# Attention steps of two batches placed in the middle of units and outputs, and their kv one unit later

## The chip, the cores and the metric

The kernel runs on one core of one Trainium2 chip. The metric is the device time in microseconds (us). A run also has a *span*, from the first to the last instruction of its trace; in most runs here the device time is 1.7 to 1.9 us above the span. "Fast" runs alone are compared. In the profile's lines PE is TensorE's products and PEld its weight loads, DVE is VectorE, ACT is ScalarE, POOL is GpSimd, and L158 is line 158 of that run's kernel.

## The reference, cut to what matters

```python
def _attn_ref(q, k, v, g_norm):            # q, k, v: 8 batches x 8 heads x 576 tokens x 64
    kv  = np.einsum('bhsd,bhse->bhde', k, v)
    out = np.einsum('bhsd,bhde->bhse', q, kv)
    rms = np.sqrt(np.mean(out * out, axis=-1, keepdims=True) + 1e-06)
    return out / rms * g_norm
# its result, as x of 4608 tokens x 512, goes through
def _moe_ref(x, w_a, w_b, w_out):          # d_ff = 1536
    return ((x @ w_a) * (x @ w_b)) @ w_out
```

Nearly all the arithmetic is in the three large products. The attention is small, but every token of x has to pass through it first.

## The kernel before

The 4608 tokens go through the large products in nine strips of 512 (`s` = 0 to 8). A strip has 12 *units* (`ffn_ab`: part a with 4 products and a ScalarE copy, part b with 4 products and a VectorE multiplication) and then 4 *outputs* (`ffn_o`: 12 products each). In strip `s`, the attention of batch `b = s + 1` is computed in *slots* between units and outputs, so that its x is ready when strip `s + 1` wants it. A batch has 4 pairs of heads, and a pair goes through these steps:

- `kv`: 40 narrow products for all four pairs at once, then `kv_out`, two ScalarE copies (their result is `kvb`);
- `x`: two 288-column products into banks 4 and 5 of PSUM, the memory that the products write to, then `psq`, the ScalarE square (its result is `sq`);
- `pss`: two 288-column products of the squares into banks 6 and 7, then ScalarE's reciprocal root (`rs`); and `pst`: two VectorE products that read banks 4 and 5 and write x.

All pairs (0 to 3) use the same banks 4 and 5, so x of one pair must wait for pst of the pair before it.

```python
    X, SS = (4, 0), 6
    # class Attn, cut
        def psq(self, p, i0):
            nc.scalar.activation(sq[p % 3], P[:, i0 : i0 + 2, 0:HF], AF.Square)
        def pss(self, p, i0, hs=(0, 1)):
            ...  # two products into banks i0, i0 + 1, then rs on ScalarE
        def pst(self, p, x0, hs=(0, 1)):
            for h in hs:
                ...
                nc.vector.scalar_tensor_tensor(out=xt[p][:, t0 : t0 + HF],
                    in0=P[:, x0 + h, 0:HF], scalar=g_col, in1=rs[p % 3][:, h, :], ...)
        def x(self, p, i0):
            for h in range(2):
                nc.tensor.matmul(P[:, i0 + h, 0:HF], lhsT=kvb[self.b % 2][:, p, :], ...)

    def slot(A, s, n):
        kb = P[:, 7, 0 : NP * D].rearrange("q (p e) -> q p e", e=D)
        k0, kn, xs = (5, 1, (7, 9, 11, 13)) if s < 3 else (2, 1, (4, 7, 10, 12))
        if k0 <= n < k0 + kn:
            for p in range((n - k0) * NP // kn, (n - k0 + 1) * NP // kn):
                A.kv(p, kb[:, p, :])
            if n == k0 + kn - 1:
                A.kv_out(slice(0, NP), kb)
        for p in range(NP):
            if n == xs[p]:
                A.x(p, X[0])
                A.psq(p, X[0])
            if n == xs[p] + 1:
                A.pss(p, SS)
                A.pst(p, X[0])

    for s in range(1, N_STRIP - 1):
        b = s + 1
        A = Attn(b) if b < B else None
        for n in range(FC + 4):
            if n >= FC:
                i = O if n % 2 == 0 else n_ab[0] % 3
                n_ab[0] += n % 2
                ffn_o(s, n - FC, i)
            elif s > 1 or n > 1:
                ffn_ab(s, n)
            if A:
                slot(A, s, n)
            ...  # loads of later batches
```

Of the kernel before, what the change touches and what calls it, by code (L numbers as in the profile page):

```python
# [15 lines left out]
def kernel(  # L16
# [18 lines left out]
    FC = d_ff // 128  # L35
    NP = H // 2
# [59 lines left out]
    O = 3  # L96
# [26 lines left out]
    def load_late(b):  # L123
        if b > EARLY:

            nc.gpsimd.tensor_copy(gate, qT[(b - 1) % 2][0:1, 0, 0:1])  # L126
        d = qs_d[b].rearrange("t (h d) -> t h d", h=H)
        for hs in (slice(0, NP), slice(NP, H)):
            nc.gpsimd.dma_start(out=d[:, hs, :], in_=q[b, hs].rearrange("h t d -> t h d"))  # L129
        n = 128 * LC  # L130
        for t, src in ((ktl[b % 2], k), (vtl[b % 2], v)):
            nc.gpsimd.dma_start(
                out=t[:, :, 0:LC, :],
                in_=src[b, :, 0:n].rearrange("h (t c) d -> t h c d", c=LC),
            )
            nc.gpsimd.dma_start(
                out=t[0 : S - n, :, LC, :], in_=src[b, :, n:].rearrange("h t d -> t h d")
            )

    def transpose_q(b):  # L140
        nc.sync.dma_start_transpose(qT[b % 2], qs_d[b])
# [102 lines left out]
    class Unit:  # L244
        n = 0
# [32 lines left out]

    n_ab = [0]

    def ffn_ab(s, fc):
        i = n_ab[0]
        n_ab[0] += 2
        Unit(s, fc, i % 3, (i + 1) % 3).rest()

    def store(t0, t, e0, e1, eng=nc.sync):
        i = 0
# [15 lines left out]
    def o_mm(s, g, i, fcs, e0=0, e1=d_model):  # L303
        for fc in fcs:
            nc.tensor.matmul(  # L305
                P[:, i, e0:e1],
                lhsT=abt[s % 2][fc][:, g * 128 : (g + 1) * 128],
                rhs=wo_t[:, fc, e0:e1],
                start=(fc == 0),
                stop=(fc == FC - 1),  # L310
            )

    def o_out(s, g, i):
        n = n_o[0]
        n_o[0] += 1
        t = o_sb[n % 4]
        if n % 2:
            nc.scalar.copy(t, P[:, i, :])  # L318
        else:
            nc.vector.tensor_copy(t, P[:, i, :])  # L320
        store(s * STRIP + g * 128, t, 0, d_model)

    def ffn_o(s, g, i=O):
        o_mm(s, g, i, range(FC))
        o_out(s, g, i)


# [41 lines left out]
    X, SS = (4, 0), 6  # L369


    A = Attn(0)
# [31 lines left out]
    for p in range(1, NP):  # L404
        i = X[p % 2]
# [38 lines left out]
    for fc in range(4, FC):  # L444
        ffn_ab(0, fc)


    A = Attn(1)
    h1, h2 = range(0, FC // 2), range(FC // 2, FC)

    nc.sync.dma_start(out=gate_d, in_=vt[1][0:1, H - 1, EC - 1, D - 1 : D])
    ffn_o(0, 0, X[0])
    pieces = [(1, h1), (1, h2), (2, h1), (2, h2), (3, h1), (3, h2)]
    for n, (g, fcs) in enumerate(pieces):
# [24 lines left out]
    def slot(A, s, n):  # L479

        kb = P[:, 7, 0 : NP * D].rearrange("q (p e) -> q p e", e=D)
        k0, kn, xs = (5, 1, (7, 9, 11, 13)) if s < 3 else (2, 1, (4, 7, 10, 12))
        if k0 <= n < k0 + kn:
            for p in range((n - k0) * NP // kn, (n - k0 + 1) * NP // kn):
                A.kv(p, kb[:, p, :])
            if n == k0 + kn - 1:
                A.kv_out(slice(0, NP), kb)
        for p in range(NP):
            if n == xs[p]:
                A.x(p, X[0])  # L490
                A.psq(p, X[0])
            if n == xs[p] + 1:
                A.pss(p, SS)
                A.pst(p, X[0])

    for s in range(1, N_STRIP - 1):
        b = s + 1
        A = Attn(b) if b < B else None
        for n in range(FC + 4):
            if n >= FC:  # L500
                i = O if n % 2 == 0 else n_ab[0] % 3
                n_ab[0] += n % 2
                ffn_o(s, n - FC, i)
            elif s > 1 or n > 1:
                ffn_ab(s, n)
            if A:
                slot(A, s, n)
            if n == 8 and b + 1 < B:
                if s > 1:
                    transpose_q(b + 1)  # L510
                    if b + 2 < B:
                        load_late(b + 2)
                else:
                    load_late(3)
        if s == 1:
            transpose_q(3)
            load_late(4)
    last = N_STRIP - 1
    for fc in range(FC):
        ffn_ab(last, fc)  # L520
    for g in range(3):
        ffn_o(last, g, (O, 4)[g % 2])
# [38 lines left out]
```

## Time and profile before

| | before |
|---|---|
| device time, median of 3 runs (range) | 322.15 us (321.6 to 322.46) |
| span of the profiled run | 320.7 us |
| PE busy, share of the span | 98% |
| VectorE, ScalarE busy | 39%, 39% |
| granted TensorE clock | 1.0 |

The head of the page of the kernel before: busy time with its share of the span and the number of instructions, and the granted clock in 40 slices (9 is 90% or more).

```profile
span 320.7 us, 4732 instructions
PE 315.0 (98%) x1883; PEld 150.6 (47%) x1883; DVE 124.9 (39%) x218; ACT 125.5 (39%) x217; POOL 70.0 (22%) x94
PEclk9999999999999999999999999999999999999999
```

PE busy at 98% does not yet say that PE is at its best. In this trace the records of products overlap: one 512-column product is recorded with 379 ns, but the next one starts 216 ns after it. The first line is that of one of the three large products in the kernel before (busy us, mean ns of one, idle us before), the other two are from its timeline (start us, duration us):

```profile
L255 PE MATMUL P<-xt,wa_t 128*128 128x512 bf16 x432 | 111.9, 379 | 0.0
64.17 1.03 PE L255 MATMUL P<-xt,wa_t 128*128 128x512 bf16 x4
65.03 1.03 PE L255 MATMUL P<-xt,wb_t 128*128 128x512 bf16 x4
```

Four products start in 65.03 - 64.17 = 0.86 us. So the question to put to each place is whether the *starts* follow each other at that rate. They do nearly everywhere. The exceptions can be found in two views. The first is PE's waits in the kernel before: who waited for whom, in total, how often, the longest.

```profile
PE P L330 <- DVE eps_t L345: 1.2, 1, 1.2
PE P L158 <- DMA vtl<-in_v_dram: 0.5, 1, 0.5
PE P L209 <- ACT sq L205: 0.4, 1, 0.4
```

The first and third are at the start, as is a fourth line of 0.2 us that is left out. The second is kv of batch 2, in strip 1, waiting for the tile `vtl` with v. The timeline of the kernel before shows it (start, duration, engine, line, what was done, how many; in brackets the idle time before it and who ended it):

```profile
60.07 1.03 PE L255 MATMUL P<-xt,wb_t 128*128 128x512 bf16 x4
61.03 0.32 PE L158 MATMUL P<-vtl,ktl 128*64 128x64 bf16 x8
61.80 0.69 PE L158 MATMUL P<-vtl,ktl 128*64 128x64 bf16 x32 [0.46 <-DMA vtl<-in_v_dram]
62.43 1.04 PE L255 MATMUL P<-xt,wa_t 128*128 128x512 bf16 x4
```

From the first kv product to the next unit's first product it takes 62.43 - 61.03 = 1.40 us. The same group in strip 2 takes 0.75 us, so 0.64 us is lost here (1.397 - 0.754 by the unrounded starts):

```profile
95.81 0.82 PE L158 MATMUL P<-vtl,ktl 128*64 128x64 bf16 x40
96.56 0.61 PE L255 MATMUL P<-xt,wa_t 128*128 128x512 bf16 x2
```

The second exception is too small for the view of waits. This is the timeline of the kernel before around x of pair 1 in strip 1:

```profile
67.86 0.41 PE L209 MATMUL P<-sq,ones 128*128 128x288 bf16 x2
68.31 0.74 ACT L213 ACTIVATE rs<-P,eps_t 128x576 f32<-128x576 f32 x1 [0.52 <-PE P L209]
69.08 0.94 DVE L223 SCALAR_TENSOR_TENSOR xt<-P,g_col,rs 128x288 bf16<-128x288 f32 x2 [0.26 <-ACT rs L213]
69.84 0.53 PE L235 MATMUL P<-qT,kvb 128*128 128x288 bf16 x2
70.20 0.81 PE L255 MATMUL P<-xt,wa_t 128*128 128x512 bf16 x3
```

pss of pair 0 starts at 67.86, rs follows, then pst until 70.02. x of pair 1 starts at 69.84, and its two products take 0.53 us where those of pss take 0.41: the second stands 0.12 us until pst has let go of bank 5. It occurs in strips 1 and 2: four times 0.123 us, read from the starts.

### The profile page before, as it was taken

What the parts mean: (1) busy time and instruction counts of PE and PEld (TensorE: products, weight loads), DVE (VectorE), ACT (ScalarE), POOL (GpSimd) and SP (SyncE); (2) the same over time, 40 slices, a digit from 0 to 9 for tenths busy, and PEclk for the clock granted to TensorE, in tenths of its full rate; (3) what the DMA queues carried; (4) which work ended last, traced back from release to release, by engine and by line L of the source; (5) the groups of instructions that cost most, each with busy time, mean ns of one, the idle gap of its engine ahead of it and who ended that gap; (6) DMA issues with size and microseconds to landing.
All of it is one profiled execution on the core that took longest, in us unless ns stands there. A gap on an engine that the chain in (4) does not pass through costs nothing.

```text
span 320.7 us, 4732 instructions
## 1 busy us (share of the span) xinstructions
PE 315.0 (98%) x1883; PEld 150.6 (47%) x1883; DVE 124.9 (39%) x218; ACT 125.5 (39%) x217; POOL 70.0 (22%) x94
## 2 busy tenths in 40 slices
PE   8999999999999999999999999999999999999995
PEld 3444454444444444444444445444444444444443
DVE  4543344344234433453244424532354243313421
ACT  3643165353335433552355325432454233123310
POOL 8944990070044080250080000000000000000000
PEclk9999999999999999999999999999999999999999
DMA  8999999999359999899799150003000200020002
GB/s 180 197 196 199 198 181 229 141 93 160 91 91 159 130 132 210 85 134 155 141 69 154 65 132 9 0 35 99 0 2 0 98 35 0 25 89 21 0 33 98
DMA packets 79308, 32.60 MB, mean 102 GB/s; under 512 B 49974, under 2 KB 74806, under 8 KB 79286
## 3 DMA queue, kind: packets, MB, share of 16 engines
q0 software_dynamic: 59120, 18.44, 52.7%
q1 hardware_dynamic: 19810, 13.44, 17.7%
q10 hardware_dynamic: 356, 0.43, 0.4%
q8 instruction: 14, 0.23, 0.3%
q14 instruction: 8, 0.07, 0.1%
HBM read 37.75 MB, written 12.98 MB: 158 GB/s over the span
## 4 chain that ended last, share of the span: by engine, by line
PE 80%; DMA 12%; POOL 6%; issue 1%; ACT 0%; POOLq 0%
PE P L255 49%; PE P L305 26%; DMA wb_t<-in_moe_w_b_dram 6%; DMA vtl<-in_v_dram 5%; PE P L235 2%; PE P L209 2%; DMA qt<-in_q_dram 2%; PE P L158 1%; POOL qs L129 1%; POOL vt L106 1%; POOL wo_t L121 1%; POOL qt L106 1%; POOL kt L106 1%; POOL wb_t L360 0%; POOL wa_t L360 0%
## 5 line engine op out<-in xcount | busy, mean ns | idle before, releaser
L273 DVE TENSOR_TENSOR ab<-P,asb 128x512 bf16<-128x512 f32 x108 | 74.5, 691 | 124.5 <-PE P L255 123.6
L255 PE MATMUL P<-xt,wa_t 128*128 128x512 bf16 x432 | 111.9, 379 | 0.0
L255 PE MATMUL P<-xt,wb_t 128*128 128x512 bf16 x432 | 111.7, 379 | 0.0
L305 PE MATMUL P<-wo_t,ab 128*128 128x512 bf16 (+1 forms) x444 | 97.9, 373 | 0.0
L269 ACT CAST asb<-P 128x512 bf16<-128x512 f32 x108 | 63.0, 585 | 81.8 <-PE P L255 80.4
L255 PEld LDWEIGHTS <-wb_t 128*128 128x128 bf16 x432 | 42.3, 98 | 51.0 <-DMA wb_t<-in_moe_w_b_dram 0.2
L305 PEld LDWEIGHTS <-ab 128*128 128x128 bf16 x444 | 43.1, 98 | 45.6
L255 PEld LDWEIGHTS <-wa_t 128*128 128x128 bf16 x432 | 41.7, 98 | 44.7 <-issue 0.5
L223 DVE SCALAR_TENSOR_TENSOR xt<-P,g_col,rs 128x288 bf16<-128x288 f32 x64 | 30.1, 512 | 24.3 <-ACT rs L213 24.3
L213 ACT ACTIVATE rs<-P,eps_t 128x576 f32<-128x576 f32 (+1 forms) x33 | 23.9, 727 | 20.8 <-PE P L209 16.5
L318 ACT COPY osb<-P 128x512 f32<-128x512 f32 x17 | 9.9, 585 | 48.6 <-PE P L305 46.8
L205 ACT ACTIVATE sq<-P 128x576 bf16<-128x576 f32 x31 | 20.1, 650 | 20.4 <-PE P L235 18.3
L320 DVE COPY osb<-P 128x512 f32<-128x512 f32 x18 | 12.4, 691 | 32.4 <-PE P L305 32.3
L129 POOL DMA_DIRECT2D qs<-in_q_dram x12 | 19.5, 1635 | 2.2 <-issue 2.1
L126 POOL COPY gate<-qT 1x1 bf16<-1x1 bf16 x5 | 0.9, 176 | 85.3 <-DMA qT<-qs 85.3
L209 PE MATMUL P<-sq,ones 128*128 128x288 bf16 x64 | 13.2, 286 | 0.5 <-ACT sq L205 0.4
L235 PE MATMUL P<-qT,kvb 128*128 128x288 bf16 x56 | 11.9, 286 | 0.0
L169 ACT CAST kvb<-P 64x256 bf16<-64x256 f32 (+1 forms) x20 | 6.0, 301 | 11.7 <-PE P L158 11.6
L209 PEld LDWEIGHTS <-ones 128*128 128x128 bf16 x64 | 6.2, 98 | 7.4 <-issue 0.4
L235 PEld LDWEIGHTS <-kvb 128*128 128x128 bf16 x56 | 5.5, 98 | 6.0
L330 PE MATMUL P<-zeros 128*128 128x512 bf16 x17 | 6.9, 547 | 1.2 <-DVE eps_t L345 1.2
L121 POOL DMA_DIRECT2D wo_t<-in_moe_w_out_dram x12 | 6.4, 531 | 6.7 <-DMA wb_t<-in_moe_w_b_dram 3.3
(55 smaller groups left out, 83.7 us busy)
## 6 DMA issues: line engine op xcount, KB each, us to landing
out_dram<-osb SPq DMA_DIRECT2D x23, 256.0 KB, 2.0
qs<-in_q_dram POOLq DMA_DIRECT2D x12, 288.0 KB, 6.4
ktl<-in_k_dram POOLq DMA_DIRECT2D x6, 512.0 KB, 8.0
vtl<-in_v_dram POOLq DMA_DIRECT2D x6, 512.0 KB, 10.0
out_dram<-osb SPq DMA_DIRECT2D x13, 128.0 KB, 2.4
wo_t<-in_moe_w_out_dram POOLq DMA_DIRECT2D x12, 128.0 KB, 5.9
wa_t<-in_moe_w_a_dram POOLq DMA_DIRECT2D x5, 256.0 KB, 9.1
wb_t<-in_moe_w_b_dram POOLq DMA_DIRECT2D x5, 256.0 KB, 9.7
```

Source lines behind the costliest of these rows:

```text
L129: nc.gpsimd.dma_start(out=d[:, hs, :], in_=q[b, hs].rearrange("h t d -> t h d"))
L205: nc.scalar.activation(sq[p % 3], P[:, i0 : i0 + 2, 0:HF], AF.Square)
L209: nc.tensor.matmul(P[:, i0 + h, 0:HF], lhsT=ones, rhs=sq[p % 3][:, h, :], start=True, stop=True)
L213: nc.scalar.activation(rs[p % 3][:, h0:h1, :], P[:, i0 + h0 : i0 + h1, 0:HF], AF.Abs_reciprocal_sqrt, bias=eps_t,)
L223: nc.vector.scalar_tensor_tensor(out=xt[p][:, t0 : t0 + HF], in0=P[:, x0 + h, 0:HF], scalar=g_col, in1=rs[p % 3][:, h, :], op0=ALU.mult, o ...
L235: nc.tensor.matmul(P[:, i0 + h, 0:HF], lhsT=kvb[self.b % 2][:, p, :], rhs=self.qT[:, p, h * HF : (h + 1) * HF], start=True, stop=True,)
L255: nc.tensor.matmul(self.a if w is wa_t else self.b, lhsT=w[:, kc, self.fc * 128 : (self.fc + 1) * 128], rhs=xt[kc][:, t0 : t0 + STRIP], st ...
L269: nc.scalar.copy(self.t, self.a)
L273: nc.vector.tensor_mul(abt[self.s % 2][self.fc], self.b, self.t)
L305: nc.tensor.matmul(P[:, i, e0:e1], lhsT=abt[s % 2][fc][:, g * 128 : (g + 1) * 128], rhs=wo_t[:, fc, e0:e1], start=(fc == 0), stop=(fc == F ...
L318: nc.scalar.copy(t, P[:, i, :])
L320: nc.vector.tensor_copy(t, P[:, i, :])
```

## The change

The intent is to give kv's data more time to land and pst more time to empty its banks, by using the middle of units and outputs as slots too. `n - 0.5` is the middle of unit or output `n`.

```diff
-    def ffn_ab(s, fc):
+    def ffn_ab(s, fc, between=None):
         i = n_ab[0]
         n_ab[0] += 2
-        Unit(s, fc, i % 3, (i + 1) % 3).rest()
+        u = Unit(s, fc, i % 3, (i + 1) % 3)
+        u.part_a()
+        if between:
+            between()
+        u.part_b()
 ...
-    def ffn_o(s, g, i=O):
-        o_mm(s, g, i, range(FC))
+    def ffn_o(s, g, i=O, between=None):
+        o_mm(s, g, i, range(FC // 2))
+        if between:
+            between()
+        o_mm(s, g, i, range(FC // 2, FC))
         o_out(s, g, i)
 ...
-        k0, kn, xs = (5, 1, (7, 9, 11, 13)) if s < 3 else (2, 1, (4, 7, 10, 12))
-        (kv at k0, x at xs[p], pss and pst at xs[p] + 1)
+        if s < 3:
+            k0, xs, ss = 6, (7, 9.5, 12, 13.5), (8, 10.5, 12.5, 14)
+        else:
+            k0, xs, ss = 2, (4, 7, 10, 12), (5, 8, 11, 13)
+        (kv at k0, x at xs[p], pss and pst at ss[p])
 ...
+            amid = (lambda n=n: slot(A, s, n - 0.5)) if A else None
-                ffn_o(s, n - FC, i)
+                ffn_o(s, n - FC, i, amid)
 ...
-                ffn_ab(s, n)
+                ffn_ab(s, n, amid)
```

(The two lines in round brackets stand for the loops that use these numbers.) Nothing is added or taken away on any engine; the order changes in strips 1 and 2 alone.

More of the change, by code (lines that the diff above doesn't have):

```diff
@@ L481, in slot @@
         kb = P[:, 7, 0 : NP * D].rearrange("q (p e) -> q p e", e=D)
-        k0, kn, xs = (5, 1, (7, 9, 11, 13)) if s < 3 else (2, 1, (4, 7, 10, 12))
-        if k0 <= n < k0 + kn:
-            for p in range((n - k0) * NP // kn, (n - k0 + 1) * NP // kn):
-                A.kv(p, kb[:, p, :])
-            if n == k0 + kn - 1:
-                A.kv_out(slice(0, NP), kb)
-        for p in range(NP):
-            if n == xs[p]:
-                A.x(p, X[0])
-                A.psq(p, X[0])
-            if n == xs[p] + 1:
-                A.pss(p, SS)
-                A.pst(p, X[0])
+        if s < 3:
+            k0, xs, ss = 6, (7, 9.5, 12, 13.5), (8, 10.5, 12.5, 14)
+        else:
+            k0, xs, ss = 2, (4, 7, 10, 12), (5, 8, 11, 13)
+        if n == k0:
+            for p in range(NP):
+                A.kv(p, kb[:, p, :])
+            A.kv_out(slice(0, NP), kb)
+        if n in xs:
+            p = xs.index(n)
+            A.x(p, X[0])
+            A.psq(p, X[0])
+        if n in ss:
+            p = ss.index(n)
+            A.pss(p, SS)
+            A.pst(p, X[0])
     for s in range(1, N_STRIP - 1):
```

## The prediction

> **What bounds the kernel now.** TensorE's stream. The page shows PE busy 315.0 of 320.7 us, but matmul ends are modelled, so I read start-to-start times in the timeline: 512-column products follow each other every 0.216 us, 288-column ones every 0.12 us, clock granted 1.0 throughout. [...] From about 22 us to the last product the stream is late only around narrow kv and transpose groups (about 0.1 us each), in one wait in strip 1, and in four small waits at x. VectorE and ScalarE are 39% busy.
>
> **What the change can take away.**
> 1. kv of batch 2 (strip 1, after unit 5): its 40 products take 1.40 us from 60.84 us, every later kv group 0.76 us. The view of waits says PE waits 0.5 us for vtl's DMA, which lands at 61.6 us. One unit later (1.73 us) kv would start at 62.57 us: gain 0.64 us.
> 2. x in strips 1 and 2: the second product of pairs 1 and 3 waits 0.123 us for the second pst that empties its bank (at 69.65, 73.71, 103.79, 107.85 us). Only one unit lies between pss and the next x, and rs (0.74 us), pst (0.94 us) and hand-offs take about 2.1 us. Afterwards 1.5 units (2.6 us) or more lie between: gain 4 x 0.123 = 0.49 us.
>
> No instruction or DMA is added or removed. Only strips 1 and 2 are reordered. Ceiling: 1.13 us, all on the critical path, since PE is.
>
> **What it could add.** Estimates from trace durations:
> - x to pss falls to half an output (1.29 us) for pairs 2 and 3. From the start of x, sq ends after 1.1 us, pss starts after 1.54: slack 0.4 us.
> - kv to x falls to one unit: kvb ends about 1.0 us after kv, x comes 1.8 us after: slack 0.7 us.
> - The tightest: pair 1's pst (middle of unit 11) stands before unit 11's VectorE product. rs waits for unit 11's ScalarE copy, so from the unit's start rs ends at 2.40, pst at 3.38, the product at 4.10 to 4.15 us. The first output's last product starts at 4.35, its weights load 0.1 to 0.2 us earlier. Slack about 0; worst about 0.1 us a strip.
> - Pair 3's pss stays after output 14, so strip 2's first units find x as before.
>
> **Prediction.** 322.15 - 1.13 + 0.1 for the tight spot = about 321.1 us. Repeats of before spread 0.86 us, nearly the gain, and the landing behind item 1 can move between executions: 8 times in 10 between 320.4 and 321.8 us. Faster by over 2%: 0.5%; within 2%: 99%; slower by over 2%: 0.5%.
>
> **What would show each step right.** Item 1: vtl is no longer among PE's releasers, and strip 1's kv takes 0.76 us. Item 2: all paired x products in strips 1 and 2 start 0.12 us apart. Added cost: the last product of the first output in strips 1 and 2 follows its predecessor by 0.216 (or up to 0.3) us. Later strips last the same to 0.1 us. The span falls from 320.7 to about 319.6 us.
>
> **What would make it wrong.** vtl landing over 1 us later than in this trace; unit 11's product later than computed; ScalarE blocked behind an output's copy so that pss waits for sq; or a spread between runs and chips that hides a third of a per cent.

The times of day in this prediction come from a list whose zero lies 0.19 us after the profile's: its 60.84 us is the profile's 61.03. The durations are not touched by that. Its item 2 names "pairs 1 and 3", a slip: the four times that it lists belong to pairs 1 and 2 (69.84, 73.90, 103.97 and 108.04 us in the profile), the pairs with a single unit between the pss before and x. Pair 3 has a whole output between and did not wait.

## The result, and the profile after

A ratio in this document is the mean time of one kernel's fast runs over that of the other's fast runs of the same rounds, so it is not quite the ratio of the medians.

| | before | after |
|---|---|---|
| device time, median of 6 runs (range) | 322.02 us (321.6 to 322.46) | 321.35 us (321.16 to 321.61) |
| ratio, with 95% interval | | 0.9979 (0.9966 to 0.9991) |
| span of the profiled run | 320.7 us | 319.4 us |

The head of the page of the changed kernel:

```profile
span 319.4 us, 4695 instructions
PE 312.0 (98%) x1848; PEld 150.2 (47%) x1883; DVE 124.6 (39%) x218; ACT 125.3 (39%) x217; POOL 70.2 (22%) x94
PEclk9999999999999999999999999999999999999999
```

The program still has 1883 products, as the count of weight loads shows; 35 records of products are missing from this trace. PE's lower busy time is therefore no gain, and idle times of 0.2 to 0.3 us that this trace gives as "issue" are such holes.

PE's waits in the changed kernel, all but two "issue" lines and one of 0.2 us at the start:

```profile
PE P L337 <- DVE eps_t L352: 1.2, 1, 1.2
PE P L209 <- ACT sq L205: 0.4, 1, 0.4
```

vtl is gone from the list. The timeline of the changed kernel at kv of batch 2:

```profile
61.59 1.03 PE L255 MATMUL P<-xt,wb_t 128*128 128x512 bf16 x4
62.55 0.82 PE L158 MATMUL P<-vtl,ktl 128*64 128x64 bf16 x40
63.30 0.39 PE L255 MATMUL P<-xt,wa_t 128*128 128x512 bf16 x1
```

All 40 products run as one group, and the next unit follows 0.75 us after its start. The last piece of vtl landed at 61.49 us in this trace, a microsecond before kv began. The timeline of the changed kernel at x of pair 1:

```profile
67.01 0.41 PE L209 MATMUL P<-sq,ones 128*128 128x288 bf16 x2
67.46 0.74 ACT L213 ACTIVATE rs<-P,eps_t 128x576 f32<-128x576 f32 x1 [0.52 <-PE P L209]
68.23 0.94 DVE L223 SCALAR_TENSOR_TENSOR xt<-P,g_col,rs 128x288 bf16<-128x288 f32 x2 [0.26 <-ACT rs L213]
69.85 0.41 PE L235 MATMUL P<-qT,kvb 128*128 128x288 bf16 x2
```

From the start of pss of pair 0 to the end of its pst it takes 69.17 - 67.01 = 2.16 us, as before (70.02 - 67.86). What changed is when x starts: 2.84 us after pss in place of 1.98 us. Both products now run without a gap (0.41 us). All eight pairs of strips 1 and 2 look like this.

The prediction named one tight spot: pst of pair 1 stands on VectorE ahead of unit 11's multiplication, which the first output's last product needs. The timeline of the changed kernel there:

```profile
72.02 0.58 ACT L269 CAST asb<-P 128x512 bf16<-128x512 f32 x1 [0.83 <-PE P L255]
72.50 0.75 ACT L213 ACTIVATE rs<-P,eps_t 128x576 f32<-128x576 f32 x1
72.71 2.47 PEld L309 LDWEIGHTS <-ab 128*128 128x128 bf16 x12
73.28 0.94 DVE L223 SCALAR_TENSOR_TENSOR xt<-P,g_col,rs 128x288 bf16<-128x288 f32 x2 [1.36 <-ACT rs L213]
74.14 0.68 DVE L273 TENSOR_TENSOR ab<-P,asb 128x512 bf16<-128x512 f32 x1
75.52 0.41 PE L235 MATMUL P<-qT,kvb 128*128 128x288 bf16 x2
```

The multiplication ends at 74.82. The weight load that reads its result is the last of the twelve and starts at 75.09, 0.215 us after the one before it (the others: 0.215 or 0.216), and x follows the output at the usual time. There was 0.27 us between them, in strip 2 too, and no wait.

To see where the time went, I compare when each strip ends, taken as the start of the copy of its last output in the timeline. The table has the change in each stretch's length, against the first profile of the kernel before:

| profile | to the end of strip 0 | strip 1 | strip 2 | strips 3 to 8 |
|---|---|---|---|---|
| after | -0.21 | -0.88 | -0.24 | 0.00 |

Strip 1: 0.64 (kv) + 2 x 0.123 (x) = 0.89. Strip 2: 2 x 0.123 = 0.25. Both agree with the table within its rounding. The -0.21 us is in the start-up, which the change does not touch and which moved by -0.2 to +0.4 us from trace to trace. So the change itself is worth 1.12 us in this pair of traces, and the medians differ by 0.67 us. The experiments have to say whether that is noise.

### The profile page after: what moved, and what is told of

Read it like the earlier page. It is cut to its first block, busy times and chain, and to the rows that moved or that the text cites. A ratio compares the mean times of both kernels' runs of the same rounds, so it can differ in the third digit from the quotient of the medians.

```text
span 319.4 us, 4695 instructions
## 1 busy us (share of the span) xinstructions
PE 312.0 (98%) x1848; PEld 150.2 (47%) x1883; DVE 124.6 (39%) x218; ACT 125.3 (39%) x217; POOL 70.2 (22%) x94
## 4 chain that ended last, share of the span: by engine, by line
PE 93%; POOL 3%; DMA 2%; issue 1%; ACT 0%; POOLq 0%
PE P L255 58%; PE P L309 29%; PE P L209 2%; PE P L235 2%; DMA wb_t<-in_moe_w_b_dram 2%; PE P L158 2%; POOL vt L106 1%; POOL qt L106 1%; POOL kt L106 1%; PE P L182 0%; POOL wa_t L367 0%; POOL wb_t L367 0%; ACT o_end L540 0%; POOL ident masks.py:199 0%; POOL ident masks.py:197 0%
## 5 line engine op out<-in xcount | busy, mean ns | idle before, releaser
L255 PE MATMUL P<-xt,wb_t 128*128 128x512 bf16 x421 | 110.1, 379 | 0.3
L337 PE MATMUL P<-zeros 128*128 128x512 bf16 x16 | 6.2, 532 | 1.2 <-DVE eps_t L352 1.2
```

Source lines behind the costliest of these rows:

```text
L255: nc.tensor.matmul(self.a if w is wa_t else self.b, lhsT=w[:, kc, self.fc * 128 : (self.fc + 1) * 128], rhs=xt[kc][:, t0 : t0 + STRIP], st ...
```

## The experiments

"Against before" means the kernel before, run on the same chip. PE's stream by stretches, in us against the first profile of before, for all the profiles:

| profile | to the end of strip 0 | strip 1 | strip 2 | strips 3 to 8 |
|---|---|---|---|---|
| before, again | -0.05 | +0.08 | -0.01 | 0.00 |
| kv only | +0.39 | -0.64 | 0.00 | 0.00 |
| x only | -0.10 | -0.05 | -0.24 | 0.00 |
| kv one unit too early | +0.05 | +3.43 | 0.00 | 0.00 |
| the same, PE kept busy | -0.06 | +1.52 | -0.01 | 0.00 |
| x close behind pss | -0.02 | +2.12 | +2.76 | 0.00 |
| after, again | +0.19 | -0.88 | -0.24 | 0.00 |
| candidate, kv merged | -0.01 | -0.88 | -0.24 | -0.22 |

### e1_kv_only: only kv moved

```diff
-        k0, kn, xs = (5, 1, (7, 9, 11, 13)) if s < 3 else (2, 1, (4, 7, 10, 12))
+        k0, kn, xs = (6, 1, (7, 9, 11, 13)) if s < 3 else (2, 1, (4, 7, 10, 12))
```

> Only kv of batches 2 and 3 one unit later; x, pss and pst stay as in the kernel before. My theory (PE waits for vtl's landing): the 0.64 us wait in strip 1 goes, the four 0.123 us waits at x stay: -0.64 us against before in every round. Rival (the profiled execution of before was an unlucky one and vtl usually lands earlier): about -0.2 us on average, and the times of before spread more widely than this kernel's. Second rival (what the two profiles showed was mostly start-up noise): 0.

Measured: 321.94 us against 322.63 us, ratio 0.9982 (0.9965 to 1.0), so about -0.58 us. In the trace, strip 1 is 0.64 us shorter and strip 2 not at all: kv's move in strip 2 is worth nothing. vtl is not among PE's waits. The interval of the times is too wide to tell -0.64 from -0.2. The spans, which leave out what lies around the program, can: their means are 320.10 us here and 320.85 us for before, so -0.75 us with a standard error of 0.16. The rival also expected the times of before to spread more widely than this kernel's, and by the spans they do (320.1 to 321.4 us against 319.9 to 320.5; the times of this kernel spread by 1.3 us themselves). So that much of the rival fits: the wait is there, but its size seems to differ between executions. The timeline of this kernel at kv of batch 2:

```profile
63.15 0.82 PE L158 MATMUL P<-vtl,ktl 128*64 128x64 bf16 x40
63.90 0.82 PE L255 MATMUL P<-xt,wa_t 128*128 128x512 bf16 x3
```

### e2_x_only: only x and pss moved

```diff
-            k0, xs, ss = 6, (7, 9.5, 12, 13.5), (8, 10.5, 12.5, 14)
+            k0, xs, ss = 5, (7, 9.5, 12, 13.5), (8, 10.5, 12.5, 14)
```

(against the changed kernel)

> Only the attention steps' new places (x and pss also in the middle of units and outputs); kv of batches 2 and 3 stays after unit 5. My theory (the second x product waits for the pst that empties its bank): the four waits of 0.123 us go, vtl's wait of about 0.5 to 0.6 us stays: -0.49 us against before. Rival (the gain was in kv alone, the x waits were shifted and not removed): 0. In the profile the tight product of unit 11 ends about 0.2 us before the weights of the first output's last product are wanted.

Measured: 322.09 us against 322.63 us, ratio 0.9983 (0.9970 to 0.9997), about -0.55 us. In the trace, strip 2 is 0.24 us shorter. Strip 1 is only 0.05 us shorter, because in this execution vtl landed 0.09 us later (61.85 against 61.76) and PE came to kv 0.10 us earlier (60.93 against 61.03), so kv waited longer. PE's wait for it in this kernel:

```profile
PE P L158 <- DMA vtl<-in_v_dram: 0.7, 1, 0.7
```

The kv group lost 0.84 us here in place of 0.64 us; 0.25 us saved at x less 0.20 us more at kv gives the 0.05. The rival, that the waits at x were only shifted, is out: all x pairs run in 0.41 us, as this one (pair 1 in strip 1):

```profile
70.79 0.41 PE L235 MATMUL P<-qT,kvb 128*128 128x288 bf16 x2
```

The tight multiplication ended 0.27 us before the weight load, where 0.2 us was expected.

### e4_x_close: x placed closer behind pss

```diff
-            k0, xs, ss = 6, (7, 9.5, 12, 13.5), (8, 10.5, 12.5, 14)
+            k0, xs, ss = 6, (7, 9, 11, 13), (8.5, 10.5, 12.5, 14)
```

(against the changed kernel)

> As the changed kernel, but in strips 1 and 2 pss follows later and the next x earlier, so that only half a unit or half an output to one lies between them. My theory: x waits until 2.2 to 2.45 us after the pss of the pair before: about 1.2 us at pairs 1 and 2, 0.55 us at pair 3, 3.0 us a strip, 6.0 us in all over the changed kernel, +4.9 us against before. Rival (the 0.123 us is a fixed cost of two products after each other and not a wait for pst): under +0.5 us against the changed kernel.

Measured: 327.4 us against 322.63 us, ratio 1.0149 (1.0134 to 1.0163), +4.8 us. The starts give waits of 1.23, 1.23 and 0.55 us a strip, as computed. The view of waits of this kernel has the four longest:

```profile
PE P L235 <- DVE xt L223: 3.0, 4, 0.8
```

The timeline of this kernel at x of pair 1:

```profile
69.53 0.94 DVE L223 SCALAR_TENSOR_TENSOR xt<-P,g_col,rs 128x288 bf16<-128x288 f32 x2 [1.36 <-ACT rs L213]
70.10 0.71 PE L235 MATMUL P<-qT,kvb 128*128 128x288 bf16 x2 [0.76 <-DVE xt L223]
```

The first x product starts once the first pst has ended, the second after the second pst (70.47). That the wait grows with what is put between shows that it is a wait for pst and not a price of two products in a row.

### e3_kv_early: kv one unit earlier

```diff
+        if s == 1:
+            k0 = 4
```

(against the kernel before)

> The kernel before with kv of batch 2 one unit earlier still (after unit 4 of strip 1), so that PE stands waiting for vtl whatever the landing does. My theory: the landing sets the end of kv, so all of the unit's 1.73 us is added to the wait: +1.7 us against before, wait about 2.3 us in the profile. Rival (before usually has no wait, vtl lands earlier than in its profile): under +1.4 us. A fixed cost of placing kv there: 0.

Measured: 325.29 us against 322.63 us, ratio 1.0077 (1.0051 to 1.0102), about +2.5 us. This is more than the wait explains, and the runs spread from 323.68 to 326.41 us. The timeline of this kernel at kv:

```profile
60.57 0.32 PE L158 MATMUL P<-vtl,ktl 128*64 128x64 bf16 x8 [1.14 <-DMA vtl<-in_v_dram]
61.87 0.69 PE L158 MATMUL P<-vtl,ktl 128*64 128x64 bf16 x32 [0.99 <-DMA vtl<-in_v_dram]
```

Its busy times by stretches (the stretch and its length; busy time and number of instructions of PE, weight loads, VectorE, ScalarE and GpSimd; the granted clock; the DMA share; GB/s):

```profile
59.00:62.00 3.00, 0.87 (x19) 0.44 (x19) 0.69 (x1) 0.19 (x1) 0.00 (x0) 1.00 1.44 159
62.00:65.00 3.00, 3.00 (x40) 1.46 (x38) 0.00 (x0) 1.32 (x3) 1.04 (x2) 0.69 0.22 49
65.00:68.00 3.00, 3.00 (x12) 1.16 (x11) 0.77 (x2) 0.59 (x1) 3.00 (x3) 0.74 0.93 59
68.00:71.00 3.00, 3.00 (x17) 1.45 (x15) 1.31 (x2) 1.55 (x3) 2.52 (x4) 1.00 1.94 126
```

The wait is as my theory said: the group lost 2.38 us by its starts, 1.74 us more than before. But after it the clock was granted at half for 3.4 us, from about 63.1 us on (the 0.69 and 0.74 of two stretches of 3 us: (0.31 + 0.26) x 3 / 0.5 = 3.4), products started every 0.43 us in place of 0.216, and that cost another 1.7 us: 1.74 + 1.7 = 3.4, the table's +3.43. Not every execution lost its clock: three of the six have a mean clock of 0.995 and spans of 324.0 to 324.5 us, the other three 0.998 to 1.0 and 321.6 to 323.1 us.

### e5_kv_early_busy: the same, with PE kept busy

```diff
         if k0 <= n < k0 + kn:
+            if s == 1:
+                dummy(10, 7)
```

(against the kernel of the last experiment; `dummy` issues products of zeros whose result nobody reads)

> As the run with kv one unit too early, but ten products of zeros (10 x 0.216 us) fill most of PE's wait for vtl in strip 1. If the extra 1.7 us of that run's profile came from the clock, which was granted at half for one stretch of 3.4 us after the idle time, then PE kept busy keeps its clock: granted clock 1.0 after kv, +1.7 us against before (all of it the wait for the landing), and the times spread by less than 1 us in place of 2.7 us. If the landing itself moved from execution to execution, the times spread as widely as before, about +2.5 us on average.

Measured: 324.04 us against 322.13 us, ratio 1.0051 (1.0027 to 1.0076), about +1.6 us. The busy times of this kernel in the same stretches:

```profile
59.00:62.00 3.00, 3.00 (x50) 1.52 (x49) 0.69 (x1) 0.07 (x1) 0.00 (x0) 1.00 1.33 185
62.00:65.00 3.00, 3.00 (x30) 1.42 (x23) 0.69 (x1) 1.36 (x4) 1.49 (x2) 1.00 0.04 10
```

The clock stays at 1.0 in these stretches (0.999 to 1.0 in the mean of each run) and the six runs lie within 0.28 us (323.98 to 324.26). With ten useless products more, this kernel has the lower ratio to before (1.0051 against 1.0077, about 0.8 us, though the intervals overlap). So the extra 1.7 us in the last experiment's trace came with the lowered clock, and the three slowest of its six runs are those with the lowest mean clock. That the landing has no part in the spread is not shown: the ten products hide the wait for it as well, and the last experiment's three runs with a clock of 0.998 or more still differ by 1.5 us. One part of my expectation missed: kv did not wait at all here, because vtl landed at 61.28 us, before the ten products were through. The +1.52 us in the trace is the products' 2.16 us less the 0.64 us of before.

### b1_before_again: the kernel before

No edit.

> The kernel before again, for a second look at its wait in strip 1. My theory (the landing is set by DMA queues that are full until then): kv waits again for vtl, 0.5 to 0.9 us more than the 0.76 us that the group takes without a wait. Rival (the first profile was unlucky): hardly any wait.

Measured: one run of 323.88 us (its state is unknown, being alone; its span is 320.7 us, so 3.2 us of it lie outside the span). The trace repeats the first one: PE waits 0.5 us for vtl, the kv group loses 0.73 us, the later strips agree to 0.01 us. The first profile was not unlucky. As for the queues, the trace of before has the DMA engines 90% busy or more in every slice from 40 to 62.1 us, where the last piece of vtl landed at 61.76 us; that fits the theory, but that full queues set the landing was not tested.

### a1_after_again and a2_after_third: the direct comparison again

No edit.

> The changed kernel again, word for word, with more rounds. The two parts measured alone gave ratios 0.9982 (kv) and 0.9983 (x), so if they add up this should give about 0.9965, -1.1 us against before. If the first direct measurement (0.9979, -0.68 us) is nearer the truth, the parts overlap or the kv part varies from execution to execution.

Measured: 321.54 us against 322.13 us, ratio 0.9977 (0.9953 to 1.0001), about -0.7 us.

> The changed kernel a third time, to settle the size: two direct measurements gave 0.9979 and 0.9977 (-0.7 us), the sum of the parts -1.13 us. Vtl's last landing lay between 61.3 and 62.2 us in nine profiles, so the wait that the change takes away should be 0.2 to 1.0 us, 0.57 us on average, and the whole gain 0.7 to 1.5 us with a mean of 1.06 us: ratio 0.9967. A ratio again at 0.9977 or above says that the kernel before waits less in its timed executions than in its profiles.

Measured: 321.37 us against 322.85 us, ratio 0.9954 (0.9942 to 0.9966), about -1.5 us. One of the six executions, the profiled one, took 849.84 us. It is in none of the comparisons; the last section says what its trace shows.

So three direct ratios are 0.9979, 0.9977 and 0.9954. To pool them I take spans, which leave out what lies around the program: the changed kernel's 17 fast runs have a mean span of 319.65 us (319.4 to 320.4), and the 33 runs of the kernel before one of 320.75 us (320.0 to 321.6). That is -1.10 us, close to the sum of the two parts in the traces. (The first six runs of before have no spans.) The spans give -0.82 us (first repeat) and -1.28 us (second), so the size is known to a few tenths only. The smaller gain of the first comparison needs no other cause than noise: start-up, the landing of vtl and the time outside the span move single runs by as much as the effect.

### c1_kv_merged: a candidate

```diff
-        if n == k0:
+        if n == k0 and s < 6:
             for p in range(NP):
                 A.kv(p, kb[:, p, :])
+            if s == 5:
+                kb2 = P[:, 7, NP * D : 2 * NP * D].rearrange("q (p e) -> q p e", e=D)
+                A2 = Attn(A.b + 1)
+                for p in range(NP):
+                    A2.kv(p, kb2[:, p, :])
             A.kv_out(slice(0, NP), kb)
+            if s == 5:
+                A2.kv_out(slice(0, NP), kb2)
```

(against the changed kernel)

> A candidate that follows from the traces: with all waits gone, what is left in TensorE's stream are the 0.1 us before and 0.1 us after each group of narrow kv products. Here kv of batch 7 follows directly on kv of batch 6 in strip 5, its data having landed 17 us before. One group fewer: strip 6 shorter by 0.96 us, strip 5 longer by 0.76 us, -0.2 us against the changed kernel in the trace, too little to be seen in the times (-1.3 us against before if the changed kernel gives -1.1). If the gaps belong to the products and not to the group: 0.

Measured: 321.33 us against 322.85 us, ratio 0.9952 (0.9940 to 0.9964); the changed kernel had 0.9954 in the same rounds. The trace shows what the times can't: strip 5 is 0.63 us longer, strip 6 is 0.85 us shorter, together -0.22 us. So it beats the kernel before clearly, and the changed kernel by the trace alone. The doubled group in this kernel:

```profile
191.43 1.46 PE L158 MATMUL P<-vtl,ktl 128*64 128x64 bf16 x80
192.82 1.04 PE L255 MATMUL P<-xt,wa_t 128*128 128x512 bf16 x4
```

From its start to the next unit's it takes 192.82 - 191.43 = 1.39 us, against 2 x 0.754 = 1.51 us for two groups. Another 0.09 us, the delay before a group's first product, falls away with the second group.

## Why the prediction was right or wrong

The predicted time was 321.1 us (320.4 to 321.8), the measured one 321.35 us: right. The gain was a little below what was said in the first comparison (-0.7 us, where -1.13 + 0.1 was forecast) and close to it over all runs (-1.10 us by the spans).

- **What bounds the kernel: right.** Apart from the start-up, only moves that shortened PE's stream showed in the span, and strips that were not reordered kept their length to 0.01 us in every profile but the slow one. The stream's rate was 216 ns for 512 columns (four products in 0.86 us); whether PE could go faster with these products was not tested.
- **kv, 0.64 us: right in mechanism and size.** Moved alone it gave 0.64 us in strip 1 and nothing in strip 2. The size is not a constant, though: vtl's last landing lay between 61.20 and 62.16 us in the ten profiles of fast or unknown state, and four profiles with kv after unit 5 or earlier lost 0.64, 0.73, 0.84 and (with 1.73 us of being early taken off, 2.38 - 1.73) 0.65 us there. With the earliest of these landings before would have lost about 0.1 us (an estimate: 0.64 less 61.76 - 61.20), so that 0.64 us came back so exactly is in part luck.
- **x, 4 x 0.123 us: right, but for the name of one pair (2, not 3).** 0.25 us a strip in each profile of the changed kernel, and the wait follows the distance to pst (1.23 us where the distance is half a unit).
- **The tight spot: the mechanism right, the slack too small.** The prediction had the multiplication end 4.10 to 4.15 us after unit 11's start, slack about 0, and put 0.1 us on the sum for it. Measured, unit 11 starts at 70.95 and the multiplication ends at 74.82: 3.87 us, 0.27 us before the weights are loaded. The mis-sized term is the hand-off between instructions of the same engine. The prediction's sum left 0.03 to 0.08 us between pst and the multiplication (4.10 to 4.15, less 3.38, less 0.69); in the trace rs starts at 72.50 while the copy before it is recorded until 72.60, and the multiplication at 74.14 while pst is recorded until 74.22, so they overlap by about 0.1 us. The trace of before could have warned me: there the two pst of a pair are recorded with 506 to 519 ns each but take 0.94 us together, an overlap of about 0.08 us.
- **The other slacks: right.** No pss waits for sq and no x for kvb in strips 1 and 2.
- **The total: right by trace, harder to see in times.** "A spread between runs and chips that hides a third of a per cent" was on the list of risks, and the first two direct comparisons show it.

Not settled: why vtl's landing moves by 0.9 us between executions. It is not needed for the result, since in the changed kernel kv starts after the latest of these landings (62.55 against 62.16 us), but by 0.4 us only. Within one trace the smallest margin was 0.58 us (x close behind pss: kv at 62.74, landing at 62.16).

## What to carry to other kernels

When the busiest engine streams at its rate, look at the starts of its instructions and not at its busy time: the two things that were wrong here, 0.64 and 0.49 us, were half invisible in the view of waits, and both were cured by placing the same instructions elsewhere. For each buffer that is reused, add up the chain that empties it (here 2.16 to 2.41 us from pss to the end of pst) and put at least that much other work between; a slot in the middle of a unit was as good here as one between units (x took 0.41 us in both). And where TensorE has to stand still in two pieces, look at the granted clock afterwards: in the profile with kv one unit too early the halved clock cost nearly as much (1.7 us) as the longer wait (1.74 us), and ten useless products in the gap avoided it (clock 1.0).

## What the traces showed beside the forecast

- In the run with kv one unit too early, two idle stretches of 1.14 and 0.99 us within 2.5 us, with eight narrow products between them, were followed by half the clock for 3.4 us (in the profiled execution; two of the other five have the same mean clock of 0.995). Single gaps of 0.76 us (x close behind pss) were not: the mean clock is 1.0 in all four runs. Ten products of zeros in the gap kept the clock at 1.0. Where the limit lies was not tested.
- A group of products with 64-column weights among those with 128-column ones costs time at both ends: in the trace of before its first product starts 0.309 us after a 512-column one in place of 0.216 (0.09 us late), and the first 128-column one after it starts 0.128 us after its last, where its own follow each other every 0.016 us in the mean (0.1 us late). Joining two groups into one saved 0.22 us in all. The reason was not tested.
- One execution of the changed kernel took 849.84 us with the same instructions. Its 512-column products are recorded with 832 to 837 ns in the mean, where the kernel before has 379, while VectorE's multiplication kept its 692 ns (691 before). The profile has no record of the clock for it (its page has no PEclk line), so the 1.0 in its list of cores is no measurement. What caused this execution is open.
